# A sliding-window attention with a feed-forward behind it: one batch's values and shift issued a group sooner, queries and keys of the later batches in one load a batch

## The chip, the cores and the metric

The kernel runs on one core of a Trainium2 chip. The metric is the device time of one execution in microseconds (us), lower is better. The core's engines are named as in the profile: PE (TensorE, matrix multiplication, with PEld for its weight loads), ACT (ScalarE), DVE (VectorE), POOL (GpSimd) and SP (SyncE). POOL and SP issue the DMAs here; "POOLq" and "SPq" are their queues.

## The reference

```
q, k, v: (8 batches, 8 heads, 576 positions, 64)
scores = q @ k.T / 8, kept where 0 <= query - key < 64, else -1e9
attn   = softmax(scores) @ v                     # per batch and head
x      = attn, heads side by side: (4608 tokens, 512)
h      = x @ w_in                                # w_in (512, 2048)
out    = (h * clip(h + 3, 0, 6) / 6) @ w_out     # w_out (2048, 512), result float32
```

So there is a causal attention over a window of 64 keys, and behind it a feed-forward layer with a hard-swish between two matrix products. Nearly all multiplications lie in the feed-forward layer.

## The kernel before, in words

Two heads form a **pair**; a batch has four pairs, and pair `t` is batch `t // 4`, group `t % 4`, 32 pairs in all. The feed-forward layer works on **blocks** of 512 tokens. Its matmuls are queued as units of four (`first_units`, L469, for `hT = w_in.T @ x`; `second_units`, L507, for the output) in the list `moe`, and `weave(n)` (L573) puts the next `n` of them into the instruction stream. Thus the attention of one batch and the feed-forward layer of the block before it share PE, in an order written out by hand. Each engine works through its own instructions strictly in that order.

The main loop (L852) runs over pairs 8 to 31, and each turn calls `group(t, n)` (L752), which emits, in this order:

- `pv(t)` (L383, matmuls at L404): masked weights of pair `t` times the values, into the PSUM tile `o`;
- `turn(t + 2)` (L269, L276): PE transposes queries and keys of the pair two ahead;
- `s_first` and `s_rest` (L291, L301): scores of pair `t + 1`; then `weights(t + 1)` (L316): exponentials on ACT (L319, L323), then three products with the window mask on POOL, one small (L328, into `P0`) and two large (L331, into `Pz`). `pv(t + 1)` needs these;
- `pv_out(t)` (L409): sums, reciprocals and scaling on DVE, and `turned` (L282): copies of the transposes out of PSUM;
- `x_(t)` (L435): DMA transposes of the result into `xT`, issued on SP (L442); `xT` is what the feed-forward layer reads;
- `weave`: feed-forward units, with ACT's L499 and DVE's L500 between the two products, and the output write on SP (L531).

Behind each group the loop issues the loads of the next batch. All loads come from POOL, which also writes their descriptors and casts float32 to bfloat16 on the way:

- `load_qk(b, n, first)` (L115, L119): keys and queries, one DMA each, of `n` pairs from pair `first` on, into a staging tile; there are two such tiles, taken in turn by the batches. With `n=1`, 144 KB each. `load_qk(b + 1, 1)` at group 0 takes the tile and loads pair 0; at groups 1, 2 and 3 the other pairs follow.
- `load_v(b, part=...)` (L131, L138): three DMAs, two of 256 KB into `Un` (the two halves of the positions) and one of 64 KB into a quarter of `Us`. The same two pairs of value tiles serve even and odd batches.
- `shift(b)` (L155, L158 and L159): two DMAs on SP that copy the values, moved by 32 partitions, from `Un` to `Us`; they need the loaded `Un`. `pv` of the batch reads `Un` and `Us`.

For batch 3 the loop issues the first large value load behind group 0 of batch 2 (pair 8), the other large one and the small one behind group 1, and the shift behind group 2. From batch 4 on all three value loads come behind group 1 and the shift behind group 2. In batch 2 a group has 16 large matmuls; in batches 3 to 6 it has more, since a second block's units are spread over it as well. At the first group of a batch from 3 on, `queue_block` (L540) adds the units of the next block; in batch 3 four leftover units of the block before stand ahead of them.

Of the kernel before, what the change touches and what calls it, by code (L numbers as in the profile page):

```python
# [36 lines left out]
def kernel(  # L37
# [13 lines left out]
    NG = H // 2  # L51
# [47 lines left out]
    def load_early_qk(pairs, first=0):  # L99
        if first:  # L100
            tiles = staged[0]
        else:
            both = stage.tile([SP, 2, H, R * D], BF16, name="qk6", tag="qk")
            tiles = [both[:, 0], both[:, 1]]
        h = 2 * first
        for n in pairs:
            for t, src in zip(tiles, (q, k)):
                nc.gpsimd.dma_start(  # L108
                    out=t[:, h : h + 2 * n, :],
                    in_=src[0, h : h + 2 * n].rearrange("h (p r) d -> p h (r d)", r=R),  # L110
                )
            h += 2 * n
        return tiles

    def load_qk(b, n=NG, first=0):  # L115
        t = staged[b] if first else stage.tile([P, H, RL * D], BF16, name="qk9", tag="qk")
        hs = slice(2 * first, 2 * (first + n))
        for z, src in enumerate((k, q)):
            nc.gpsimd.dma_start(  # L119
                out=t[halves[z], hs], in_=src[b, hs].rearrange("h (p r) d -> p h (r d)", r=RL)  # L120
            )
        return t
# [8 lines left out]
    def load_v(b, whole=False, part=slice(None)):  # L131
        loads = (
            (0, Un[b % 2][:, 0], 2 * P), (2 * P, Un[b % 2][:, 1], 2 * P),
            *(((W, Us[b % 2][:, 0], 2 * P), (W + 2 * P, Us[b % 2][:, 1], 2 * P)) if whole
              else ((4 * P, Us[b % 2][3 * P // 4 : P, 1], W),)),
        )
        for m, to, n in loads[part]:
            nc.gpsimd.dma_start(  # L138
                out=to[:, :, VO : VO + P],
                in_=v[b, :, m : m + n, :].rearrange("h (p r) d -> p h (r d)", r=2),  # L140
            )
# [13 lines left out]
    def shift(b):  # L155

        un, us = Un[b % 2], Us[b % 2]
        nc.sync.dma_start(out=us[0 : P - 32], in_=un[32:P])  # L158
        nc.sync.dma_start(out=us[P - 32 : P, 0], in_=un[0:32, 1])  # L159
# [380 lines left out]
    def queue_block(kb, kept=2 * NG, lead=2):  # L540

        f = first_units(kb)
        moe.extend(left[:lead])
        del left[:lead]
        n = len(left)
        for i, unit in enumerate(f):
            moe.extend(left[i * n // NFC : (i + 1) * n // NFC])
            moe.append(unit)
        left[:] = second_units(kb)
        n = len(left) - kept  # L550
        moe.extend(left[:n])
        del left[:n]
# [117 lines left out]
    staged = {0: load_early_qk((1,))}  # L670
# [81 lines left out]
    def group(t, n):  # L752

        if t >= 2 * NG:
            pv(t)
        if t + 2 < T:
            turn(t + 2)
        if t + 1 < T:
            host = t + 2
            if host >= T:  # L760
                hosts[host] = [ps_h.tile([P, 8 * P], BF16, name=name, tag="bk") for name in ("tk", "tq")]
            s = s_first(t + 1, host)
            weights(t + 1, s, s_rest(t + 1))
        if t >= 2 * NG:
            pv_out(t)
        if t + 2 < T:
            turned(t + 2, 0)
        if t >= 2 * NG:
            x_(t)
        weave(2)  # L770
        if t + 2 < T:
            turned(t + 2, 1)
        weave(n - 2)
# [75 lines left out]
    pads(3, nc.gpsimd.memset)  # L849
    group(2 * NG - 1, 4)  # L850
    load_qk(2, 1, 3)
    for t in range(2 * NG, T):  # L852
        b, g = divmod(t, NG)
        if g == 0 and b > 2:
            queue_block(b - 1, lead=4 if b == 3 else 2)
        group(t, -(-len(moe) // (NG - g)))
        if b + 1 < B:
            if g == 0:
                staged[b + 1] = load_qk(b + 1, 1)
            else:  # L860
                load_qk(b + 1, 1, g)
            if b == 2 and g < 2:
                load_v(b + 1, part=(slice(0, 1), slice(1, 3))[g])
            if b > 2 and g == 1:
                load_v(b + 1)
            if g == 2:
                shift(b + 1)
    late[0] = 2
    queue_last(NTB - 2)
# [36 lines left out]
```

## Time and profile before

| what | value |
|---|---|
| time, median of 3 runs | 323.65 us (323.15 to 324.26) |
| the profiled execution's own time | 324.27 us |
| its span, first to last instruction | 322.5 us |
| PE busy | 306.2 us, 95% |
| DVE, ACT, POOL busy | 180.7, 184.2, 138.1 us |
| mean granted TensorE clock | 0.989 |

All starts are in microseconds from the start of the span. A line of the timeline or the chain has a start and a length, then engine, line of the kernel, operation, tiles written and read, and how many instructions were merged; in brackets the idle time of the engine before it and what ended it. A line of the waits names who waited for whom, with the total, the number of waits and the longest. A window line has the busy time with the count of instructions, the granted clock as a share of full speed, the share of time that the DMA engines were busy, and GB/s. A line of DMA issues has the number, the size and the median time from issue to landing.

Pair 8's `pv` is at 68.30 us, pair 12's (the first of batch 3) at 87.86, where it stops after two matmuls and goes on at 89.91. Batches 3 to 6 then take about 32.5 us each, up to about 250 us; the feed-forward layer of the last blocks fills the rest.

### The profile page before, as it was taken

The page shows a single profiled execution, that of the slowest core. Times are in us where ns is not written, and L with a number is a line of the kernel's source. Part 1 is how long each engine was busy: PE and PEld are TensorE (multiplying, and loading weights), DVE is VectorE, ACT ScalarE, POOL GpSimd, SP SyncE. Part 2 cuts the span into 40 slices and gives each one's busy share as a digit, 9 for nine tenths or more (in the row PEclk, how much of TensorE's full clock was granted, in tenths as well). Part 3 has the DMA queues.
Part 4 walks back from the last instruction along what each step waited for, and adds up shares of the span by engine and source line. Part 5 has one row for each costly group of instructions (what it writes and reads, how often), then busy time and mean ns, then how long its engine had stood idle before and what let it go on. Part 6 is the DMA issues. An engine that isn't in the chain of part 4 may idle for free.

```text
span 322.5 us, 10757 instructions
## 1 busy us (share of the span) xinstructions
PE 306.2 (95%) x4608; PEld 152.4 (47%) x4608; DVE 180.7 (56%) x415; ACT 184.2 (57%) x345; POOL 138.1 (43%) x192
## 2 busy tenths in 40 slices
PE   7789998999989999999999999999999999999991
PEld 3454454545445455555555555555544444444440
DVE  6666657588527762776277627762676156334200
ACT  2737574588537764776477637773774356454410
POOL 8971206289954744475548555754330000000000
PEclk9999999999979999999999999999999999999997
DMA  6999999939963966299539963996011200100021
GB/s 92 164 210 199 207 189 149 203 46 131 176 140 85 128 141 135 43 161 154 126 59 143 171 133 48 151 162 130 16 54 52 83 33 0 68 33 34 36 84 55
DMA packets 57976, 35.67 MB, mean 111 GB/s; under 512 B 40256, under 2 KB 52032, under 8 KB 57920
## 3 DMA queue, kind: packets, MB, share of 16 engines
q0 software_dynamic: 36288, 18.81, 45.5%
q1 hardware_dynamic: 21632, 16.08, 19.3%
q8 instruction: 38, 0.62, 0.8%
q14 instruction: 18, 0.15, 0.1%
HBM read 37.62 MB, written 9.44 MB: 146 GB/s over the span
## 4 chain that ended last, share of the span: by engine, by line
PE 83%; DMA 5%; POOL 5%; ACT 2%; DVE 1%; issue 1%; POOLq 0%; SPq 0%; ACTq 0%
PE hT L487 35%; PE acc L523 35%; DMA V<-in_v_dram 3%; PE o L404 3%; PE acco L523 2%; PE s L310 2%; PE tk L276 2%; DMA V<-V 2%; POOL qk L108 2%; POOL Pz L331 1%; ACT t L499 1%; POOL qk L119 1%; PE tq L276 1%; POOL V L127 1%; PE hTo L487 1%
## 5 line engine op out<-in xcount | busy, mean ns | idle before, releaser
L500 DVE SCALAR_TENSOR_TENSOR gT<-t,hT 128x512 bf16<-128x512 bf16 x141 | 95.7, 687 | 79.2 <-ACT t L499 78.5
L487 PE MATMUL hT<-xT,win 128*128 128x512 bf16 x564 | 133.0, 379 | 1.3 <-DVE gT L500 0.8
L523 PE MATMUL acc<-wout,gT 128*128 128x512 bf16 x544 | 129.9, 381 | 0.0
L499 ACT ACTIVATE t<-hT,half_const 128x512 bf16<-128x512 f32 x141 | 95.8, 690 | 48.5 <-PE hT L487 47.7
L487 PEld LDWEIGHTS <-win 128*128 128x128 bf16 x576 | 55.6, 98 | 66.7 <-issue 2.0
L523 PEld LDWEIGHTS <-gT 128*128 128x128 bf16 x576 | 54.7, 98 | 63.9 <-issue 1.1
L331 POOL TENSOR_TENSOR Pz<-e,band 128x512 bf16<-128x512 bf16 x48 | 54.2, 1146 | 0.0
L328 POOL TENSOR_TENSOR P<-e,first 64x256 bf16<-64x256 bf16 x24 | 15.9, 663 | 77.4 <-ACT e L319 77.4
L529 ACT COPY osb<-acc 128x512 f32<-128x512 f32 x34 | 19.9, 586 | 44.2 <-PE acc L523 44.0
L323 ACT ACTIVATE e<-s 128x512 bf16<-128x512 f32 x56 | 30.1, 590 | 0.2 <-issue 0.2
L283 DVE COPY KT<-tk 128x576 bf16<-128x576 bf16 x28 | 21.0, 750 | 5.3 <-ACT e L319 4.5
L138 POOL DMA_DIRECT2D V<-in_v_dram x22 | 17.8, 823 | 9.5 <-DMA win<-in_moe_w_in_dram 4.6
L428 DVE TENSOR_TENSOR opl<-o,recs 128x256 bf16<-128x256 f32 x52 | 19.7, 420 | 0.5
L413 DVE TENSOR_REDUCE sums<-o 128x10 f32<-128x20 f32 x26 | 4.6, 175 | 25.5 <-PE o L404 25.5
L283 ACT COPY QT<-tq 128x576 bf16<-128x576 bf16 x28 | 17.8, 637 | 1.5 <-PE tq L276 1.5
L404 PEld LDWEIGHTS <-Pz 64*64 64x64 bf16 x1008 | 11.9, 109 | 14.3 <-issue 12.2
L119 POOL DMA_DIRECT2D qk<-in_k_dram x26 | 16.7, 644 | 1.3 <-issue 1.3
L319 ACT ACTIVATE e<-tk 64x128 bf16<-64x128 f32 x28 | 7.6, 271 | 16.4 <-PE tq L296 16.4
L404 PE MATMUL o<-V,Pz 64*64 64x65 bf16 x936 | 14.2, 197 | 2.0 <-DMA V<-V 1.8
L119 POOL DMA_DIRECT2D qk<-in_q_dram x26 | 16.0, 614 | 0.0
L310 PE MATMUL s<-QT,KT 64*64 64x64 bf16 x896 | 14.5, 196 | 0.4 <-DVE gT L500 0.4
L276 PE MATMUL tk<-ident,qk 64*64 64x64 bf16 x504 | 14.0, 197 | 0.0
(102 smaller groups left out, 203.0 us busy)
## 6 DMA issues: line engine op xcount, KB each, us to landing
out_dram<-osb SPq DMA_DIRECT2D x36, 256.0 KB, 2.5
V<-in_v_dram POOLq DMA_DIRECT2D x16, 256.0 KB, 6.0
qk<-in_q_dram POOLq DMA_DIRECT2D x28, 144.0 KB, 3.9
qk<-in_k_dram POOLq DMA_DIRECT2D x28, 144.0 KB, 3.3
V<-V SPq DMA_DIRECT2D x6, 432.0 KB, 4.3
wout<-in_moe_w_out_dram POOLq DMA_DIRECT2D x2, 1024.0 KB, 17.7
win<-in_moe_w_in_dram POOLq DMA_DIRECT2D x2, 512.0 KB, 8.3
win<-in_moe_w_in_dram POOLq DMA_DIRECT2D x1, 1024.0 KB, 12.4
```

The lines of the kernel that those rows point to most:

```text
L119: nc.gpsimd.dma_start(out=t[halves[z], hs], in_=src[b, hs].rearrange("h (p r) d -> p h (r d)", r=RL))
L276: nc.tensor.transpose(out=hosts[t][z][halves[h], r * W : (r + 1) * W], in_=staged[b][halves[z], 2 * g + h, r * D : (r + 1) * D], identity= ...
L283: (nc.scalar.copy if z else nc.vector.tensor_copy)(out=(QT[t % 4][:] if z else KT[t % 4][:, W:]).rearrange("q (p r) -> q p r", r=RL), in_= ...
L310: nc.tensor.matmul(ss[h][halves[i], c, m, r], lhsT=keys(t, h, W * (w - 1), r), rhs=QT[t % 4][halves[h], w * W : (w + 1) * W], start=True, ...
L323: nc.scalar.activation(out=e[:].rearrange("p c m r w -> p (c m r w)"), in_=ss[h][:].rearrange("p c m r w -> p (c m r w)"), func=EXP, scale ...
L331: muls[h].tensor_tensor(out=Pw[t % 4][:, h].rearrange("p c m r w -> p (c m) (r w)"), in0=e[:].rearrange("p c m r w -> p (c m) (r w)"), in1 ...
L404: nc.tensor.matmul(o[i][halves[c], c0 : c0 + D + 1], lhsT=p, rhs=vt[:, hh, v0 : v0 + D + 1], start=(r == 0), stop=(r == 1), skip_group_che ...
L487: nc.tensor.matmul(hT, lhsT=win16[:, g, fc * P : (fc + 1) * P], rhs=xT[:, g, t0 : t0 + TB], start=(g == 0), stop=(g == NG - 1),)
L499: nc.scalar.activation(out=t1[:], in_=hT, func=RELU, bias=half_const[:], scale=1.0 / 6.0)
L500: nc.vector.scalar_tensor_tensor(out=gT[:, fc, :], in0=t1[:], scalar=1.0, in1=hT, op0=MIN, op1=MULT)
L523: nc.tensor.matmul(acc, lhsT=gT[:, fc, ts * P : (ts + 1) * P], rhs=wout16[:, fc, :], start=(fc == 0), stop=(fc == NFC - 1),)
L529: nc.scalar.copy(out=osb[:], in_=acc)
```

## The change

```diff
@@ -849,6 +849,7 @@
     pads(3, nc.gpsimd.memset)
     group(2 * NG - 1, 4)
     load_qk(2, 1, 3)
+    load_v(3, part=slice(0, 2))
     for t in range(2 * NG, T):
         b, g = divmod(t, NG)
         if g == 0 and b > 2:
@@ -856,14 +857,14 @@
         group(t, -(-len(moe) // (NG - g)))
         if b + 1 < B:
             if g == 0:
-                staged[b + 1] = load_qk(b + 1, 1)
-            else:
+                staged[b + 1] = load_qk(b + 1, NG if b > 2 else 1)
+            elif b == 2:
                 load_qk(b + 1, 1, g)
-            if b == 2 and g < 2:
-                load_v(b + 1, part=(slice(0, 1), slice(1, 3))[g])
+            if b == 2 and g == 0:
+                load_v(b + 1, part=slice(2, 3))
             if b > 2 and g == 1:
                 load_v(b + 1)
-            if g == 2:
+            if g == 1 + (b > 2):
                 shift(b + 1)
     late[0] = 2
     queue_last(NTB - 2)
```

Batch 3: its two large value loads are issued ahead of the loop, behind the last query and key load of batch 2; the small one follows behind group 0 of batch 2, and the shift behind group 1 in place of group 2. The queries and keys of batch 3 still come pair by pair.

Batches 4 to 7: behind group 0 of the batch before, one key load and one query load bring all four pairs (576 KB each); the loads behind groups 1, 2 and 3 are gone. Values and shift keep their groups. No instruction on PE, ACT or DVE is added, removed or reordered.

## The prediction

> **What bounds the kernel now.** I read the page first, then the chain that ended last in order of time, then the waits between 66 and 100 us, and last the busy time and granted clock in half-microsecond windows.
>
> ```profile
> span 322.5 us, 10757 instructions
> ...
> PE 306.2 (95%) x4608; PEld 152.4 (47%) x4608; DVE 180.7 (56%) x415; ACT 184.2 (57%) x345; POOL 138.1 (43%) x192
> ...
> PE 83%; DMA 5%; POOL 5%; ACT 2%; DVE 1%; issue 1%; POOLq 0%; SPq 0%; ACTq 0%
> ```
>
> TensorE (PE) is the bound, so only what makes PE wait, or run at a lower clock, can be won. Next, a window over most of batches 3 to 7; the columns are length, PE busy (count), granted clock, DMA share, GB/s.
>
> ```profile
> 97.00:250.00 153.00, 152.60 (x2626) 1.00 0.64 110
> ```
>
> In 153 us PE is idle for 0.4, at full clock. The second half of the change (one load of queries and keys a batch) acts here, and can gain at most those 0.4 us. Before 97 us it is different:
>
> ```profile
> 77.63 1.17 POOL qk L119 x2
> 78.80 5.39 DMA V<-in_v_dram
> ...
> 84.40 5.47 DMA V<-V
> ...
> 90.12 0.70 PE o L404 x37
> ```
>
> ```profile
> PE o L404 <- DMA V<-V: 1.8, 1, 1.8
> ```
>
> That is the chain, and then the list of waits. Batch 3's value load leaves GpSimd (POOL) at 78.80, the shift (`V<-V`, L158) waits for it and leaves at 84.40, and the first `pv` of batch 3 (pair 12, L404) waits for the shift's landing, 1.8 us. It is PE's only wait for a transfer in that stretch. What came of it stands in the windows:
>
> ```profile
> 88.00:88.50 0.50, 0.08 (x2) 1.00 0.75 190
> ...
> 90.00:90.50 0.50, 0.48 (x30) 0.69 1.15 191
> 90.50:91.00 0.50, 0.50 (x53) 0.50 1.19 198
> ...
> 93.00:93.50 0.50, 0.50 (x3) 0.50 0.00 0
> 93.50:94.00 0.50, 0.50 (x4) 0.90 0.34 67
> ```
>
> At the end of the gap the granted clock falls to 0.50 and stays until about 93.5. The price is the sum of length times (1 - clock): 0.5 x 0.31 + six windows x 0.25 + 0.5 x 0.10 = 1.70 us. The stall so costs nearly twice what the list of waits shows.
>
> **The change part by part.** First PE's and POOL's timelines through batch 2. Columns: start, length, line, operation, count, and in brackets the idle time before.
>
> ```profile
> 68.30 0.45 PE L404 MATMUL o<-V,Pz 64*64 64x65 bf16 x32
> 72.95 0.45 PE L404 MATMUL o<-V,Pz 64*64 64x65 bf16 x32
> 77.77 0.45 PE L404 MATMUL o<-V,Pz 64*64 64x65 bf16 x32
> 79.33 1.89 PE L487 MATMUL hT<-xT,win 128*128 128x512 bf16 x8 [0.20 <-DVE gT L500]
> 82.88 0.76 PE L404 MATMUL o<-V,Pz 64*64 64x65 bf16 x32
> 89.91 0.80 PE L404 MATMUL o<-V,Pz 64*64 64x65 bf16 x30 [1.83 <-DMA V<-V]
> ```
>
> ```profile
> 68.01 0.65 POOL L119 DMA_DIRECT2D qk<-in_k_dram  x1
> 68.66 0.60 POOL L119 DMA_DIRECT2D qk<-in_q_dram  x1
> 69.74 0.66 POOL L328 TENSOR_TENSOR P<-e,first 64x256 bf16<-64x256 bf16 x1 [0.48 <-ACT e L319]
> 70.37 2.26 POOL L331 TENSOR_TENSOR Pz<-e,band 128x512 bf16<-128x512 bf16 x2
> ...
> 73.81 0.91 POOL L138 DMA_DIRECT2D V<-in_v_dram  x1
> 74.72 0.69 POOL L328 TENSOR_TENSOR P<-e,first 64x256 bf16<-64x256 bf16 x1
> ...
> 78.80 1.49 POOL L138 DMA_DIRECT2D V<-in_v_dram  x2
> 80.30 0.69 POOL L328 TENSOR_TENSOR P<-e,first 64x256 bf16<-64x256 bf16 x1
> ```
>
> A group of batch 2 lasts 4.65 us (72.95 - 68.30). In that time POOL masks the next pair's weights (0.66 + 2.26) and issues a key and a query load (0.65 + 0.60): 4.2 us, so it has under 0.5 us to spare, and value loads issued on it push the next masks back. That is so today: the masks at 74.72 and 80.30 have no idle time before them. A large value load (256 KB) costs 0.91 to issue; of the two at 78.80 the other is the small one (64 KB), 1.49 - 0.91 = 0.58.
>
> *Removed: the stall.* The two large loads now come behind the query load that ends at 69.26, so they are issued from 69.26 to 71.08 and not from 73.81 and 78.80. With the old 5.39 from issue to landing the second, leaving at 70.2, lands near 75.6.
>
> ```profile
> 77.02 1.23 SPq L442 DMA_TRANSPOSE xT<-opg  x1
> ...
> 84.40 0.54 SPq L158 DMA_DIRECT2D V<-V  x1
> ```
>
> The shift now stands on SyncE's queue (SP) behind pair 9's transposes, which end at 78.25, or about 79.4 with the 1.1 us found below. It is one pair earlier than before, and the value load no longer holds it. It lands at 79.4 + 5.47 = 84.9; its second piece and the small value load come within a microsecond or so. PE needs them near 88.5. Even if the shift also waited for the small load (issued about 75.8, landing about 81.2 by the same 5.39), it would land at 86.7. So the 1.83 us go, and with them the cause of the 1.70 us at half clock: **-3.53 us**.
>
> *Added: POOL is late a group sooner.* Pair 9's mask could start at 69.74. It now starts at 71.08 and its second product ends 1.34 later than at 72.63, at 73.97. PE reaches pair 9's `pv` at 72.95 and waits about 1.1 us (0.3 were slack): **+1.1 us**. If each issue took the 0.58 of the small load it would be +0.4, and no row is longer than 0.91. Behind that `pv` on PE's queue stand pair 11's transposes, pair 10's scores and all the group's large matmuls, so the wait is paid in full.
>
> *Given back later.* One group on, POOL has the small load (0.58) and not a large one (0.91), then none where two stood (1.49). Pair 11's mask no longer waits for POOL's issues, and the stretched `pv` at 82.88 (0.76, against 0.45 elsewhere) should be whole again: -0.31. The wait of 0.20 at 79.33 on a PSUM bank may go too, since ScalarE and VectorE catch up during PE's wait: **-0.5 us** in all. The least is nothing. The most is all that lies over 4.65 a group from 72.95 to PE's arrival at 88.08 (89.91 - 1.83): 15.13 - 13.95 = 1.2.
>
> *Moved beside other transfers.* Each pair of queries is loaded two groups ahead and is barely in time.
>
> ```profile
> qk<-in_q_dram POOLq DMA_DIRECT2D x1, 144.0 KB, 4.3
> qk<-in_q_dram POOLq DMA_DIRECT2D x1, 144.0 KB, 5.2
> ```
>
> The first row is the query load of 68.66, with no value load ahead of it; the second is one beside the shift (issued 83.78). The one for pair 12, issued about 74.6, now has two value loads before it; the one for pair 13, issued about 79.2, now meets the shift. With 5.2 they land at 79.8 and 84.4, while PE wants them right behind the `pv` of pairs 10 and 11, near 79.2 (77.77 + 1.0 + 0.45) and 84.0 (82.88 + 0.6 + 0.45): 0 to 1.0 us in all (0.6 + 0.4), which I put at **+0.2 us**, since half a microsecond of difference is within the spread of these landings. The Trainium skill, "DMA: Bandwidth & Descriptors" (Issuing engines are not separate DMA queues), speaks against the change here: DMAs of all issuing engines run on the same 16 DMA engines and interleave. The two rows (4.3 and 5.2) agree with it; were the loads in order by queue and not shared, this term would be 0.
>
> *One load a batch.* On POOL eight issues a batch become two, four times (batches 4 to 7).
>
> ```profile
> 20.46 0.66 POOL L119 DMA_DIRECT2D qk<-in_k_dram  x1
> ...
> 128.96 0.64 POOL L119 DMA_DIRECT2D qk<-in_k_dram  x1
> ...
> 134.25 0.66 POOL L328 TENSOR_TENSOR P<-e,first 64x256 bf16<-64x256 bf16 x1 [4.04 <-ACT e L319]
> ```
>
> ```profile
> 30.00:30.50 0.50, 0.50 (x4) 1.00 1.22 205
> ```
>
> ```profile
> 140.86 0.44 PE o L404 x40
> ```
>
> The issue at 20.46 is for two pairs at once and takes as long as one for one pair. For four pairs the cost lies between 0.66 and 4 x 0.64 = 2.6 each; I take 0.7, the nearer row. Two at 2.6 end 5.2 us after 128.96, at 134.2, just where the next mask starts, so POOL hides either. The transfer is 8 x 144 KB = 1.18 MB; at the 205 GB/s of the third row that is 5.8 us. One pair's landing of 4.3 above holds 0.7 us of moving by the same rate, so 3.6 of other time; with 0.7 for the issue ahead of it the last byte is there after some 10.1 us. The first reader is pair 20's transpose, right behind the `pv` at 140.86: 12.3 us after the issue. The load hides behind two groups of PE work with 2 us to spare: **0**, and the cost is 0 up to there, bounded by the rival below. The transposes and output writes that it slows down in that time are not read until the next batch.
>
> Sum: -3.53 + 1.1 - 0.5 + 0.2 = **-2.73 us**. The profiled execution took 324.27 us (span 322.5 and 1.77 around it), 0.62 above the median of the three runs shown (323.65). Its own forecast is 321.54; for the median I take **320.9**.
>
> **The rivals.**
>
> *The new wait drops the clock as the old one did.* The old gap of 1.83 did it. Against that stands the start of the kernel, where PE was idle for about a microsecond at full clock:
>
> ```profile
> 9.50:10.00 0.50, 0.00 (x0) 1.00 1.12 152
> 10.00:10.50 0.50, 0.00 (x0) 1.00 1.42 183
> ```
>
> So the bound lies between about 1.0 and 1.83, and the new wait of 1.1, with small matmuls around it, is near its lower end. Price: another 1.70, giving 322.6. The Trainium skill, "TensorE: Matmul & The Clock Gate" (Why this matters for your kernels), warns only of idle gaps over about 3 us. By it this rival would be impossible and the old fall unexplained; the measured fall after 1.83 us decides against it.
>
> *A transfer takes the stall's place.* The pair 12 or 13 queries, or pair 11's transposes for block 2 (PE now gets there some 3 us sooner), are late by the full 1.0 and a little more: 321.9. For it, there is no slack in the query landings; against it, each is only tenths late by the rows above.
>
> *Slower: the whole-batch load is late.* Its place is the first pair's transpose two groups on, its point a landing later than 12.3 us after issue. Each microsecond beyond costs four times, once a batch: 13.3 us would give 320.9 + 4 = 324.9, and with the clock falling each time 331.7. For it: one pair's landing of 5.2 us, taken four times, would be over the point. Against it: most of a landing is not moving, and 205 GB/s was held.
>
> *The change doesn't do what it says.* The shift keeps waiting for something else and lands near 88 or later: 323.6.
>
> **How the numbers follow.** Forecast 0.68; clock falls 0.12; late transfer 0.10; late batch load 0.07; no effect 0.03. The forecast's terms at their ends give -3.53 + 0.4 - 1.2 = -4.3 (319.3) and -3.53 + 1.1 + 1.0 = -1.4 (322.2); both ends together are unlikely, so the range is 319.6 to 322.7, which takes in the first two rivals. 0.3% is about what a measurement of this kernel can tell from no change, 322.7 and 324.6. Of the clock rival half counts as same, of the late transfer a fifth: faster 0.82, same 0.11, slower 0.07.
>
> **What would show it.** Right: no wait of `pv` on `V<-V` near 88 us and no window of clock 0.5 behind it; a wait of about 1.1 us of pair 9's `pv` on L331; the shift issued near 79; PE busy from 97 on as before. Wrong: a clock of 0.5 near 74 to 80, a PE wait on `qk`, on `xT` or, once a batch, on the single load.

## The result, and the profile after

| | kernel before | changed kernel |
|---|---|---|
| median of 22 runs each | 324.01 us (322.59 to 327.33) | 322.29 us (320.84 to 323.99) |
| ratio, 95% interval | | 0.9945 (0.9924 to 0.9965) |
| profiled execution, span | 324.27, 322.5 us | 320.98, 319.3 us |
| mean granted clock in it | 0.989 | 0.997 |

Faster by 0.55% (0.35 to 0.76%), about 1.8 us (1.1 to 2.5). The forecast was 2.7 us, to 320.9. The two profiled executions differ by 3.3, more than either. Below, "the stretch" is the time from the start of pair 8's `pv` to the start of pair 13's, which holds all of batch 2 and the place of the old stall; "the rest" is from there to the end of the span. Executions more than 1.5% above the fastest of their kernel count as disturbed and are left out of all ratios and counts, and so is the profile of the experiment with nine extra matmuls, which was one of them.

The page of the changed kernel: the same bound, with the share of DMA in the chain down from 5% to 3%.

```profile
span 319.3 us, 10688 instructions
...
PE 84%; POOL 5%; DMA 3%; ACT 2%; DVE 2%; issue 2%; POOLq 0%; ACTq 0%; DVEq 0%
```

Waits of PE between 60 and 100 us in the changed kernel (total, number, longest). The wait on `V<-V` is gone; two new ones stand in its place, on the mask and on the queries of one pair.

```profile
PE o L404 <- POOL Pz L331: 0.8, 1, 0.8
...
PE tq L276 <- DMA qk<-in_q_dram: 0.6, 1, 0.6
```

Its timelines of PE, POOL and SP in that place:

```profile
67.99 0.45 PE L404 MATMUL o<-V,Pz 64*64 64x65 bf16 x32
...
72.65 0.26 PE L404 MATMUL o<-V,Pz 64*64 64x65 bf16 x8
...
73.68 0.39 PE L404 MATMUL o<-V,Pz 64*64 64x65 bf16 x24 [0.78 <-POOL Pz L331]
...
83.82 0.45 PE L404 MATMUL o<-V,Pz 64*64 64x65 bf16 x32
...
88.56 0.45 PE L404 MATMUL o<-V,Pz 64*64 64x65 bf16 x32
...
96.80 0.45 PE L404 MATMUL o<-V,Pz 64*64 64x65 bf16 x32
```

```profile
68.93 1.79 POOL L138 DMA_DIRECT2D V<-in_v_dram  x2
70.72 0.70 POOL L328 TENSOR_TENSOR P<-e,first 64x256 bf16<-64x256 bf16 x1
...
93.09 0.74 POOL L119 DMA_DIRECT2D qk<-in_k_dram  x1
93.82 0.70 POOL L119 DMA_DIRECT2D qk<-in_q_dram  x1
```

```profile
79.33 0.54 SPq L158 DMA_DIRECT2D V<-V  x1
```

The two value loads hold pair 9's mask back (no idle time before 70.72), and `pv` of pair 9 is cut in two by 0.78 us: its first 8 matmuls run at 72.65, the others wait. Pair 11's `pv` at 83.82 has its usual 0.45 again. Pair 12's, at 88.56, is not interrupted: the shift left at 79.33. The windows (length, PE busy, granted clock, DMA share, GB/s) show full clock both in the new wait and where the old fall was:

```profile
73.00:73.50 0.50, 0.00 (x0) 1.00 1.55 149
...
90.00:90.50 0.50, 0.48 (x3) 1.00 0.60 78
```

The DMA issues by size (count, KB each, median time to landing) show the whole-batch loads in time for their readers:

```profile
qk<-in_k_dram POOLq DMA_DIRECT2D x4, 576.0 KB, 7.0
qk<-in_q_dram POOLq DMA_DIRECT2D x4, 576.0 KB, 9.5
```

The stretch fell from 31.36 to 28.81 us (-2.55), the rest from 222.84 to 222.50.

### The profile page after: what moved, and what is told of

Its sections match the earlier page's. It is cut to its first block, busy times and chain, and to the rows that moved or that the text cites. A ratio compares the mean times of both kernels' runs of the same rounds, so it can differ in the third digit from the quotient of the medians.

```text
span 319.3 us, 10688 instructions
## 1 busy us (share of the span) xinstructions
PE 302.0 (95%) x4566; PEld 151.8 (48%) x4608; DVE 181.3 (57%) x415; ACT 184.3 (58%) x345; POOL 124.3 (39%) x168
## 4 chain that ended last, share of the span: by engine, by line
PE 84%; POOL 5%; DMA 3%; ACT 2%; DVE 2%; issue 2%; POOLq 0%; ACTq 0%; DVEq 0%
PE acc L523 36%; PE hT L487 35%; PE o L404 3%; PE s L310 2%; PE acco L523 2%; PE tk L276 2%; DMA V<-in_v_dram 2%; DMA qk<-in_q_dram 2%; POOL qk L108 2%; POOL Pz L331 1%; PE tq L276 1%; ACT t L499 1%; POOL V L138 1%; POOL qk L119 1%; PE hTo L487 1%
## 5 line engine op out<-in xcount | busy, mean ns | idle before, releaser
L523 PE MATMUL acc<-wout,gT 128*128 128x512 bf16 x520 | 126.4, 379 | 2.2 <-issue 1.3
L276 PE MATMUL tq<-ident,qk 64*64 64x64 bf16 x504 | 13.9, 195 | 0.6 <-DMA qk<-in_q_dram 0.6
L276 PEld LDWEIGHTS <-qk 64*64 64x64 bf16 x1008 | 11.6, 106 | 2.9 <-issue 2.1
```

Of the source, the lines that this page charges most:

```text
L276: nc.tensor.transpose(out=hosts[t][z][halves[h], r * W : (r + 1) * W], in_=staged[b][halves[z], 2 * g + h, r * D : (r + 1) * D], identity= ...
L523: nc.tensor.matmul(acc, lhsT=gT[:, fc, ts * P : (ts + 1) * P], rhs=wout16[:, fc, :], start=(fc == 0), stop=(fc == NFC - 1),)
```

## The experiments

The theory going in: all of the gain comes from batch 3's values and shift, in two parts, the wait and the clock that falls behind it; the whole-batch loads bring nothing. The rivals: the loads carry part of it; the fall of the clock has nothing to do with the wait; the value load alone, without the shift's move, would have done. Each ratio is to the kernel before on the same chip. An edit is shown against the changed kernel unless the text names the kernel before.

**Values and shift sooner alone.**

```diff
-                staged[b + 1] = load_qk(b + 1, NG if b > 2 else 1)
-            elif b == 2:
+                staged[b + 1] = load_qk(b + 1, 1)
+            else:
                 load_qk(b + 1, 1, g)
```

> Batch 3's values and shift a group sooner alone; queries and keys of all later batches still pair by pair. Theory (the whole gain comes from the values and the shift; the whole-batch loads bring nothing): within 0.3 us of the changed kernel, a ratio to the kernel before of 0.991 to 0.996; the wait of pv on the shift near 88 us and the windows at clock 0.5 behind it are gone, the wait of pair 9's pv on its mask (0.8 us) and the wait on pair 12's queries are there as in the changed kernel. Rival (the whole-batch loads carry a part of the gain): ratio over 0.997, with PE idle between 97 and 250 us that the changed kernel has not.

Ratio 0.9927 (0.9900 to 0.9954). The stretch is 28.94 us, with the mask's wait (0.8) and the queries' (0.8, against 0.6) as in the changed kernel. This half carries the gain of the stretch.

**One load a batch alone.** The kernel before with the `load_qk` lines of the changed one.

> One load a batch for the queries and keys of batches 4 to 7 alone; values and shift of batch 3 where they were. Theory: ratio 1.000 within 0.002; the 1.8 us wait on the shift near 88 us and the clock of 0.5 behind it stay; the key and query loads of 576 KB are issued in 0.7 us each and land within 7 to 10.5 us, before the 12.3 us at which they are read. Rival: faster by 0.3% or more, from GpSimd's issues that are saved, or slower, with one PE wait a batch on the single load.

Ratio 0.9957 (0.9925 to 0.9989), against the theory. The profile had a surprise: the old wait is there, and the clock does not fall.

```profile
89.93 0.65 PE L404 MATMUL o<-V,Pz 64*64 64x65 bf16 x30 [1.77 <-DMA V<-V]
...
98.25 0.45 PE L404 MATMUL o<-V,Pz 64*64 64x65 bf16 x32
```

```profile
88.00:90.00 2.00, 0.23 (x4) 1.00 1.14 130
90.00:92.00 2.00, 1.80 (x113) 1.00 1.15 264
```

The same wait as in the kernel before, 1.77 us against 1.83, at a granted clock of 1.00 throughout; the stretch is 29.94 us. So the fall does not belong to every such wait. The new theory: the wait comes in every execution, the fall only in some.

**The changed kernel with the shift back behind group 2.**

```diff
-            if g == 1 + (b > 2):
+            if g == 2:
                 shift(b + 1)
```

> The changed kernel with batch 3's shift back behind group 2 of batch 2; the values stay a group sooner. Theory (the shift's place on SyncE's queue sets the end as much as the load does): the shift is issued behind pair 10's transposes, near 84.7 us and not 79.3, lands 5.5 us later near 90.2, so pair 12's pv at 88.6 waits about 1.5 us and the clock falls behind it: 1.5 plus 0 to 1.7 us slower than the changed kernel, near or above the time of the kernel before (ratio 0.998 to 1.003). Rival (the value load alone was the cause): the wait is gone and the time is that of the changed kernel, ratio 0.9945.

Ratio 0.9984 (0.9957 to 1.0012). The shift leaves at 86.25 us, and pair 12 waits for it:

```profile
91.52 0.64 PE L404 MATMUL o<-V,Pz 64*64 64x65 bf16 x30 [1.58 <-DMA V<-V]
```

The stretch is 30.51 us, with both the new wait on the mask and the old one on the shift, the clock again at 1.00. The load alone gains nothing here; the shift's place on SP's queue must move with it.

**Extra matmuls in the stall.** Ten matmuls of zeros ahead of pair 12's `pv`, whose result nothing reads, in the kernel before; first tried with nine.

```diff
         group(t, -(-len(moe) // (NG - g)))
+        if t == 2 * NG + 3:
+            warm(ps_t, 10)
```

> The kernel before with nine extra 128x512 matmuls of zeros into a spare PSUM bank ahead of pair 12's pv; they add 1.9 us of PE work in the place where PE waits for the shift, and their result is not read. Theory (half of the price of the stall is the clock that falls because PE is idle): the shift lands at the same time, the granted clock stays at 1.00 from 88 to 94 us, and the kernel is 1.5 to 1.8 us faster than before although it does more work, ratio 0.994 to 0.996. Rival (the clock falls for another reason, or the dip costs little): ratio 1.000 or above.

> The kernel before with ten extra matmuls of zeros (2.16 us of PE work, result not read) ahead of pair 12's pv. Theory (the granted clock falls only where PE stands idle long enough, and in the kernel before that is the wait on the shift): if the shift lands 1.8 to 2.0 us after PE gets there, as in four profiles so far, the wait on it is at most 0.3 us, the clock is 1.00 from 85 to 97 us, the stretch from pair 8's pv to pair 13's pv is 29.9 to 30.3 us, and the mean granted clock over the runs is that of the changed kernel, 0.994. Rival (it falls whatever PE does there): windows below 0.99 between 85 and 97 us, mean clock 0.990.

Nine: ratio 0.9989 (0.9959 to 1.0018). Ten: 0.9990 (0.9962 to 1.0018). The profile with ten is as the theory has it:

```profile
87.81 2.32 PE L665 MATMUL wt<-zeros 128*128 128x512 bf16 x10
90.06 0.50 PE L404 MATMUL o<-V,Pz 64*64 64x65 bf16 x32
```

No wait on the shift, no window below full clock, stretch 29.92. More PE work in the same place costs no more than the idle wait did (29.94 to 30.20 in the two executions of one load a batch alone, where the clock stayed). The mean granted clock of its 12 runs is 0.994, as the theory has it, against 0.991 in the kernel before. But the time did not fall as a certain saving of 1.5 us would have it. In 4 of the 12 runs the mean clock was below 0.992. This bound is a rough count of the executions with a fall anywhere: the five profiles used here in which the clock falls while PE works have means of 0.988 to 0.990, the eight others 0.994 to 0.998.

**The kernel before, once more.**

> The kernel before, profiled once more. Theory (the wait on the shift comes in every execution, the fall of the clock behind it in most but not all): a wait of 1.6 to 2.0 us; a stretch from pair 8's pv to pair 13's pv of 31.2 to 31.8 us if windows behind it are at 0.5, of 29.8 to 30.3 if none is. Rival (the fall is certain): 31.4 with the fall at the same place.

325.77 us, a wait of 2.11 and the fall behind it; the second window is the one at half clock.

```profile
91.43 0.62 PE L404 MATMUL o<-V,Pz 64*64 64x65 bf16 x30 [2.11 <-DMA V<-V]
```

```profile
90.00:92.00 2.00, 0.55 (x39) 1.00 1.03 128
92.00:95.00 3.00, 2.67 (x92) 0.51 0.84 238
```

Stretch 31.78, rest 222.84.

**The changed kernel and one load a batch alone, both once more.**

> The changed kernel once more, beside the others of this call on one chip. Theory (the gain has two parts: about 1.1 us from the wait on the shift, net of the new wait on the mask, in every execution, and about 1.4 us from the granted clock that falls behind the long wait, only in those executions in which it does fall): from pair 8's pv to pair 13's pv 28.8 us within 0.3; mean granted clock over all runs higher than that of the kernel before by 0.003 to 0.005; ratio 0.992 to 0.995. Rival (the whole 2.7 us come in every execution): ratio 0.990 to 0.992.

> One load a batch alone, once more. Theory (it does nothing; the 0.4% measured first came from the executions in which the clock happened to stay up): ratio above 0.997, the stretch from pair 8's pv to pair 13's pv 29.9 us where the clock stays and 31.4 where it falls, as in the kernel before. Rival (saved issues or calmer transfers bring something of their own): ratio 0.993 to 0.997 again, with the clock below 0.99 in fewer of its runs than in those of the kernel before.

The changed kernel: ratio 0.9930 (0.9905 to 0.9955), stretch 28.61. One load a batch alone: 0.9979 (0.9950 to 1.0007), a wait of 1.91 with the clock at 1.00, stretch 30.20. The first ratio lies within the theory's expectation, but its interval takes in the rival's as well. The mean granted clock of the changed kernel's runs is above that of the kernel before by 0.003 (0.9943 against 0.9912).

The profiles now make a table. It sorts by what was changed, not by chip or run:

| kernel | wait on the shift | clock falls there | the stretch | the rest |
|---|---|---|---|---|
| before | 1.83 | yes | 31.36 | 222.84 |
| before, again | 2.11 | yes | 31.78 | 222.84 |
| ten extra matmuls | none | no | 29.92 | 222.88 |
| one load a batch alone | 1.77 | no | 29.94 | 222.45 |
| the same, again | 1.91 | no | 30.20 | 222.39 |
| shift back | 1.58 | no | 30.51 | 222.37 |
| values and shift alone | none | no | 28.94 | 222.91 |
| changed kernel | none | no | 28.81 | 222.50 |
| changed kernel, again | none | no | 28.61 | 222.46 |

The last column answers the question of the whole-batch loads: 222.84 to 222.91 us in the four profiles with loads pair by pair, 222.37 to 222.50 in all with one load a batch. That is 0.4 us in every profile. Of it 0.09 us is the pace of pairs 13 to 31 (146.41 us in the kernel before, 146.32 with one load a batch alone). The larger part lies behind the last output copy, which ends 5.85 us before the end of the span in the kernel before (316.65 of 322.5) and 5.54 with one load (315.16 of 320.7). There SP's queue waits for PE's; first the kernel before, then one load a batch alone:

```profile
SPq L901 <- PEq L901: 1.0, 2, 0.8
```

```profile
SPq L901 <- PEq L901: 0.7, 2, 0.5
```

What PE's queue does in that time the profile does not show.

The count of runs with a mean clock below 0.992: the kernel before 52 of 78, the changed kernel 4 of 28, values and shift alone 2 of 6, nine extra matmuls 3 of 10, ten 4 of 12; one load a batch alone 7 of 17, the shift back 5 of 12. Without the long idle wait such runs are fewer, but not gone: in the profile of values and shift alone the clock fell at 11 us, in that of the changed kernel, again, at 9 us, both in the kernel's start. The last two of the list keep the wait on the shift and still have fewer such runs than the kernel before; why, no run shows.

**GpSimd later still.** Two extra writes into a tile that nothing reads.

```diff
+    idle = consts.tile([P, TB], BF16, name="idle")
...
     load_v(3, part=slice(0, 2))
+    for _ in range(2):
+        nc.gpsimd.memset(idle[:], 0.0)
```

> The changed kernel with two extra GpSimd writes (1.0 to 1.2 us in all, into a tile that nothing reads) behind the two value loads, ahead of pair 9's mask. Theory (GpSimd's lateness there is paid by PE in full): the wait of pair 9's pv on its mask grows from 0.8 to 1.8 to 2.0 us and the stretch from pair 8's pv to pair 13's pv from 28.7 to 29.5 to 29.9 us, with 1.4 to 1.7 on top where the clock falls. Rival (later slack takes it back, as pair 10's and 11's masks then wait less): the stretch grows by less than 0.4 us.

Ratio 0.9976 (0.9943 to 1.0008). The writes take 1.15 us; the wait of pair 9's `pv` is now in two pieces, 1.76 in all (lines are one later here):

```profile
74.41 0.26 PE L405 MATMUL o<-V,Pz 64*64 64x65 bf16 x8 [0.91 <-POOL Pz L332]
...
75.52 0.39 PE L405 MATMUL o<-V,Pz 64*64 64x65 bf16 x24 [0.85 <-POOL Pz L332]
```

From pair 8's `pv` to pair 10's it is 11.38 us against 10.34 in the changed kernel: +1.04 for 1.15. Up to there PE pays GpSimd's lateness nearly in full; up to pair 11's `pv` it is 0.7 and 0.9 us more than in the two profiles of the changed kernel, still above the rival's 0.4. The whole stretch, 31.88, says less: it holds another wait of 1.9 us in pair 12's scores, to which the last experiment comes back. The clock stayed at 1.00.

**All value loads a group sooner still.**

```diff
     pads(3, nc.gpsimd.memset)
+    load_v(3)
     group(2 * NG - 1, 4)
     load_qk(2, 1, 3)
-    load_v(3, part=slice(0, 2))
...
-            if b == 2 and g == 0:
-                load_v(b + 1, part=slice(2, 3))
```

> The changed kernel with all three value loads of batch 3 issued one group sooner still, ahead of the group in which GpSimd otherwise waits nearly 7 us for work; the shift stays where the change put it. Theory (the cost of the change is GpSimd's 1.8 us of value issues ahead of pair 9's mask): the wait of pair 9's pv on its mask (0.8 us) is gone, as is the wait on pair 12's queries (0.6); the stretch from pair 8's pv to pair 13's pv is 27.4 to 28.0 us, 0.8 to 1.4 less than the changed kernel's 28.8. Rival (the mask is late for another reason, or the wait only moves on): the stretch stays at 28.5 or above.

Ratio 0.9904 (0.9878 to 0.9930), median 321.43 us against 321.97 of the changed kernel beside it. The loads fall into time in which GpSimd had nothing to do, and pair 9's mask again waits only for the exponentials:

```profile
60.05 2.38 POOL L138 DMA_DIRECT2D V<-in_v_dram  x3
66.89 0.66 POOL L328 TENSOR_TENSOR P<-e,first 64x256 bf16<-64x256 bf16 x1 [4.46 <-ACT e L319]
...
71.46 0.66 POOL L328 TENSOR_TENSOR P<-e,first 64x256 bf16<-64x256 bf16 x1 [0.47 <-ACT e L319]
```

No wait on a mask, on queries or on the shift; the stretch is 27.73 us, 0.9 to 1.1 less than the changed kernel's. This version is the fastest that was run; its interval overlaps the changed kernel's, while the stretch of its one profile lies below both of the changed kernel's. In that profile the clock fell once, at 17 us, in the kernel's start.

**All of batch 3's loads there.**

```diff
     pads(3, nc.gpsimd.memset)
-    group(2 * NG - 1, 4)
     load_qk(2, 1, 3)
-    load_v(3, part=slice(0, 2))
+    load_v(3)
+    staged[3] = load_qk(3)
+    group(2 * NG - 1, 4)
...
-            if g == 0:
-                staged[b + 1] = load_qk(b + 1, NG if b > 2 else 1)
-            elif b == 2:
-                load_qk(b + 1, 1, g)
-            if b == 2 and g == 0:
-                load_v(b + 1, part=slice(2, 3))
+            if g == 0 and b > 2:
+                staged[b + 1] = load_qk(b + 1)
```

> As the one before, and the last queries and keys of batch 2 and all of batch 3's (one load) are issued there too, so that GpSimd issues no load in batch 2 at all. Theory: no PE wait on a mask, on queries or on the shift in batch 2, groups of 4.65 to 4.8 us, the stretch from pair 8's pv to pair 13's pv 27.0 to 27.6 us, ratio to the kernel before 0.986 to 0.990. Rival (the burst of 2.1 MB ahead of batch 2 delays batch 2's own values, their shift or its last queries): a new PE wait at pair 8's or pair 9's pv or at pair 11's transposes, and no gain over the version with the values alone.

> The version that issues all of batch 3's loads and the last of batch 2's ahead of batch 2, once more, for the one wait of PE (1.4 us in pair 10's scores, ended by nothing that the profile shows) that spoiled it the first time. If that wait belongs to this order of loads (the burst of 2 MB is still moving when PE gets there), it is there again within a group of the same place and the stretch from pair 8's pv to pair 13's pv is 29 us or more. If it was chance, as the like wait of 1.9 us in another version, it is not there, the stretch is 27.4 to 27.7 us and this version is level with the one that moves the values alone.

Ratios 0.9963 (0.9935 to 0.9992) and 0.9970 (0.9939 to 1.0002), stretches 29.09 and 30.49. The forecast rival holds in kind: no gain over the values alone. But the waits are of another sort. The first run, then the second:

```profile
75.69 0.41 PE L310 MATMUL s<-QT,KT 64*64 64x64 bf16 x27 [1.35 <-issue]
```

```profile
71.32 0.41 PE L310 MATMUL s<-QT,KT 64*64 64x64 bf16 x27 [1.78 <-issue]
...
77.24 0.41 PE L310 MATMUL s<-QT,KT 64*64 64x64 bf16 x27 [1.08 <-issue]
```

PE stops in the middle of a pair's scores, at the same place of a group each time (27 of the matmuls are left), and the profile names nothing that it waits for, which it calls "issue". In the first run VectorE's last product, the one that frees a PSUM bank, had ended at 74.31 us, before the stop began. In the two profiles of the changed kernel there is no such wait of this size; the version with the late GpSimd has one, of 1.9 us, without the burst of loads.

The DMA view holds something that fits all four stops: a queue named "instruction", which moves blocks of 16 KB. This is its line for 71 to 77 us of the first run (blocks, MB, share of the DMA engines' time):

```profile
q8 instruction: 2, 0.03, 3.7%
```

The first of the two leaves 4.6 us after the start of pair 8's `pv`; in every profile without a stop in pair 10's scores it leaves 2.0 to 3.0 us after it. Its transfer ends at 74.39, and PE goes on 1.3 us later. Ahead of the other three stops, too, a block left late: 3.3 to 4.4 us later than in the changed kernel, counted from pair 8's `pv`, of which earlier delays of PE make at most 1.8. There PE went on 1.3 to 1.6 us after the block's end. The stops fall on the same one of PE's weight loads in both runs, or 128 or 256 of them away from it, and in batch 2 of the changed kernel a block leaves about every 130 of them. So PE most likely waited for its own instructions. No experiment tests that, nor whether the queued loads made the blocks late.

## Why the prediction was right, point by point

- **The stall goes with the load and the shift together**: right. The shift left at 79.33 (forecast 79.4), and with the shift back at its old place the wait came back (1.58 us).
- **The half clock, -1.70 us**: the mechanism was right, the size was not. The sum counted as certain what one profile showed. A fall costs about 1.4 us (31.36 and 31.78 with it, 29.94 and 30.20 without, less the 0.1 by which the waits themselves differ). By the count of clocks, which takes in falls elsewhere, two runs of three had one before and one of seven after, so the mean saving is an estimated (0.67 - 0.14) x 1.4 = 0.7 us. This is the mis-sized term, and the main reason why the profiled pair differs by 3.3 us and the medians by 1.7.
- **The bound for the fall, "between about 1.0 and 1.83 us"**: wrong as a bound. Waits of 1.58, 1.77 and 1.91 us passed at full clock and one of 1.83 did not. The length does not decide alone.
- **GpSimd late, +1.1**: right in kind, 0.78 us measured. The mask ended 1.0 us after PE reached pair 9's `pv`, as the prediction's own rows give, but the first 8 matmuls (0.26 us) did not wait for it. The run with 1.15 us more showed that PE pays nearly all of it.
- **Given back, -0.5**: as forecast, pair 11's `pv` is whole again and the wait of 0.20 on VectorE's `gT` is gone.
- **Moved beside other transfers, +0.2**: pair 12's queries took the 5.2 us feared and cost 0.6 in the first profile; pair 13's took 3.4 and cost nothing.
- **One load a batch, 0**: the issues took 0.74 and 0.70 us (0.7 forecast), and the query load was there 9.4 to 11.1 us after the key load's issue (10.1 forecast), before the 12.3. The term itself was -0.4, mostly behind the last output copy, a place that the prediction has no term for.

Without the clock the stretch fell by 1.4 us (30.07 to 28.71, means of two profiles each), where the forecast's terms give 1.0. With 0.7 for the clock and 0.4 for the loads that makes 2.5, the upper edge of the first measurement (1.1 to 2.5) and inside the second (1.5 to 3.1). That this comes near the forecast's 2.7 is in part luck: the clock's term was 1.0 too large, the others together 0.8 too small. What the Trainium skill's clock page ("TensorE: Matmul & The Clock Gate", What's actually happening) says of a free-running window of 3413 ns, which is not tied to the kernel's start, would explain why equal waits end differently: whether a wait falls into one window or across two is then chance. The lengths at half clock agree (3.4 us in each of the five profiles with a fall); the window itself no run here shows.

## What to carry to other kernels

When a load is issued sooner, look at the queue that it enters: here the same two instructions took a wait of 1.8 us away and set up one of 0.8, which went too once they were moved into idle time of that queue. A drop of the clock behind a stall in one profile is a cost with a chance, so take a second profile, or the granted clock of all runs, before putting it into a sum. Compare stretches between fixed points of the program: 0.4 us were plain in "the rest" of single profiles, where ratios over 17 runs left them open. Where PE stops at "issue", the times of the blocks on the instruction queue are worth reading.

## What was not expected of the hardware

- Waits of PE of 1.77 and 1.91 us left the granted clock at 1.00; waits of 1.83 and 2.11 at the same place of the program were followed by 3.4 us at 0.5.
- With about 2 MB of loads queued ahead of batch 2, PE stopped for 1.1 to 1.8 us in the middle of a pair's scores, waiting for nothing that the profile names. Each time a 16 KB block of the queue "instruction" was late and ended 1.3 to 1.6 us before PE went on; that this was the cause is not tested.
- With 24 load DMAs fewer the end of the program, behind the last output copy, was 0.3 us shorter in every profile (5.5 to 5.6 us against 5.8 to 5.9).
